# A fused attention and gated-MLP kernel: issue order and PSUM banks from a fixed table instead of a build-time search

## Chip, cores and metric

One core of one Trainium2 chip. The metric is device time in microseconds (us) for one execution; the kernel before takes 921.35 us, the median of three runs (919.81 to 922.08). "fp32r" in the rows is the float32 form that most matmuls use here; a value is split into a rounded high part and the rest as a low part, and products of the parts are added.

## What is computed

```python
def _attn_ref(q, k, v):                       # 4 x 8 heads, 1152 keys, head size 64
    q_pool = q.reshape(B, H, S // 2, 2, D).mean(axis=3)
    scores = (1 / sqrt(D)) * q_pool @ k.T     # 576 queries per head
    scores = scores - max(scores, axis=-1)
    attn = exp(scores) / (sum(exp(scores)) + 1e-09)
    return attn @ v
def _moe_ref(x, w_gate, w_val, w_out):        # 2304 tokens, 512 -> 1536 -> 512
    return (1 / (1 + exp(-(x @ w_gate))) * (x @ w_val)) @ w_out
```

`x` is the attention output with the heads of one batch side by side. Everything is float32 at the interface.

## The kernel before, in words

Work is cut by batch (4), head (32, numbered u) and half of the queries (2 halves of 288 columns, called g). For every head: Q and K are loaded (L442, L439), two queries are added (L455), Q and K are rounded to a high part on ScalarE (L460, L475), the low parts are made on GpSimd or VectorE (L465, L481). A first product of the high parts (`maxima`, L504; `first_head`, L412 for head 0) serves only to find each query's maximum: VectorE reduces every 128x384 block of it (L510, L417), and the negated maxima become a diagonal matrix (L335, L338) that is part of the second operand pair. Then comes the true score product, two matmuls of 288 columns per chunk of 128 keys (L610), and the exponential on ScalarE (L614).

In heads 0 to 7 (`WHOLE`) the exponentials stay in float32 and go straight into the value product (L628). In heads 8 to 31 the exponential is taken twice, rounded into `eh` (L614) and unrounded into the bank itself (L643), VectorE subtracts the two into `el` (L646), and the value product is one matmul for each (L653, L657); the sum of the exponentials is collected on GpSimd (L675, L682, L685), split (L723, L726) and multiplied with ones on TensorE (L730). The pair of heads is then normalised (L748 to L757) and split into `x` (L767, L771).

After a batch's heads comes its gated MLP (`gated`), whose products are 12 matmuls of 288 columns each (L846): gate and value per 128 features (tanh on L889, product on L895, split on L899 and L903), then three passes over the output weights (L929, L931) and the store (L942). The weights are converted once, during the first batch's MLP and the heads before it (`convert`, L785 to L811), stored to DRAM and loaded again for every batch (L862). The MLP of batch b is interleaved with the attention of batch b+1, so that TensorE always has something to do; only the last batch's MLP stands alone at the end.

At the start TensorE has 18 warm-up steps of four matmuls of 128x192 on constants (L951), whose results nobody reads. They have no input but `sel` (L990, L991).

The order of all this isn't written out. `Plan.op` registers 7153 steps, each with an engine, a planned duration, a due time and what it comes after: 3141 for TensorE, 1703 for ScalarE, 1348 for VectorE, 624 for GpSimd, 337 for the SyncE queue (loads and stores). A `Hold` is a use of a buffer slot by a group of steps; `SLOTS` says how many slots a tag has. The tag `b` is the eight PSUM banks, one of which a step must take before its first matmul; 1448 holds share them. `Plan.run` is a list scheduler over these steps: it keeps a clock and a busy time for each engine, lets each engine start the ready step that is due first, makes a step visible to other engines a fixed latency later (`LAT`), and gives a taken bank the slot that has been free longest. `Plan.search` repeats it 30 times with shaken due times and keeps the earliest end. The kernel then issues every step in the order found:

```python
    order = pl.search(30, 30.0, 1.0)
    with tc.manual_schedule():
        for o in order:
            o.fn()
```

Each engine works through its own instructions strictly in that order. The waits between engines are added when the program is built, from what each instruction reads and writes; so another order changes which waits there are, not what is computed.

Of the kernel before, what the change touches and what calls it, by code (L numbers as in the profile page):

```python
# [3 lines left out]

# [16 lines left out]

class Op:
    def __init__(self, eng, dur, fn, prio, after=(), take=None, late=0.0, keep=0.0, behind=None):
        self.eng, self.dur, self.fn, self.prio = eng, dur, fn, prio
        self.after = [a for a in after if a is not None]
        self.take, self.late, self.keep = take, late, keep
        self.users, self.start, self.end, self.behind, self.next = [], None, None, behind, []


class Hold:


    def __init__(self, tag, first=None):
        self.tag, self.slot, self.ops = tag, None, []


class Plan:


    WAIT = 0.4
    LAT = {"PE": 0.2, "ACT": 0.16, "DVE": 0.14, "POOL": 0.1, "SP": 0.0}

    def __init__(self, slots, free_order=()):
        self.free_order = free_order
        self.ops = []
        self.slots = slots
        self.holds = {t: [] for t in slots}
# [4 lines left out]
        return h  # L54

    def op(self, eng, dur, fn, prio, after=(), uses=(), take=(), late=0.0, keep=0.0, behind=None):
        o = Op(eng, dur, fn, prio, after, list(take), late, keep, behind)
        for h in uses:
            if behind is None:
                o.after.append(h.ops[0])  # L60
        for h in list(take) + list(uses):
            h.ops.append(o)
        self.ops.append(o)
        return o

    def search(self, rounds, width, shift):
        dice = random.Random(1)
        best = self.run()
        end = max(o.end for o in best)
        made = [(o, o.start, o.end) for o in best]  # L70
        slots = [(h, h.slot) for hs in self.holds.values() for h in hs]
        for _ in range(rounds):
            at = dice.uniform(-width, end)
            near = [(o, o.prio) for o, s, _ in made if at <= s <= at + width and o.eng != "SP"]
            for o, p in near:
                o.prio = p + dice.uniform(-shift, shift)
            order = self.run()
            new = max(o.end for o in order)
            if new <= end:
                best, end = order, new  # L80
                made = [(o, o.start, o.end) for o in best]
                slots = [(h, h.slot) for hs in self.holds.values() for h in hs]
            else:
                for o, p in near:
                    o.prio = p
        for o, a, b in made:
            o.start, o.end = a, b
        for h, s in slots:
            h.slot = s
        return best  # L90

    def run(self):
        n_dep = {}
        ready = {e: [] for e in self.LAT}
        for o in self.ops:
            o.users, o.next = [], []
        for k, o in enumerate(self.ops):
            o.key = (o.prio, k)
            o.at = 0.0
            n_dep[o] = len(o.after)  # L100
            for a in o.after:
                a.users.append(o)
            if o.behind:
                n_dep[o] += 1
                o.behind.next.append(o)
        free = {t: [(0.0, s) for s in range(n)] for t, n in self.slots.items()}
        nxt = {t: 0 for t in self.slots}
        left, of = {}, {}
        for t, hs in self.holds.items():
            for k, h in enumerate(hs):  # L110
                h.k, h.end = k, 0.0
                left[h] = len(h.ops)
                for o in h.ops:
                    of.setdefault(o, []).append(h)
        for o in self.ops:
            if n_dep[o] == 0:
                heapq.heappush(ready[o.eng], (o.key, o))
        busy = {e: 0.0 for e in self.LAT}
        done, order, t = 0, [], 0.0
        times = [0.0]  # L120
        heapq.heapify(times)
        seen = set()

        def can(o, t):
            for h in o.take:
                n = sum(g.tag == h.tag for g in o.take) if h.tag in self.free_order else 1
                if (h.tag not in self.free_order and nxt[h.tag] != h.k) or sum(f <= t + 1e-9 for f, _ in free[h.tag]) < n:
                    return False
            return True

        while done < len(self.ops):
            if not times:
                left = sorted((o.key[0], o.eng) for e in ready for _, o in ready[e])
                raise RuntimeError(f"planner stuck at {t}: {left[:10]} {nxt}")
            t = heapq.heappop(times)
            while times and times[0] <= t + 1e-9:
                heapq.heappop(times)
            again = True
            while again:
                again = False  # L140
                for e in self.LAT:
                    if busy[e] > t + 1e-9:
                        continue
                    put, pick, soon = [], None, []
                    while ready[e]:
                        it = heapq.heappop(ready[e])
                        o = it[1]
                        if o.at <= t + 1e-9 and can(o, t):
                            pick = o
                            break  # L150
                        if t < o.at <= t + self.WAIT and can(o, o.at):
                            soon.append(o)
                        put.append(it)

                    if pick and e != "PE" and any(
                        t + pick.dur > u.at + self.WAIT and u.prio < pick.prio - 0.3 for u in soon
                    ):
                        heapq.heappush(ready[e], it)
                        pick = None
                    for it in put:  # L160
                        heapq.heappush(ready[e], it)
                    if pick is None:
                        continue
                    o = pick
                    for h in o.take:
                        h.slot = min((s for s in free[h.tag] if s[0] <= t + 1e-9), key=lambda s: s[0])[1]
                        free[h.tag] = [s for s in free[h.tag] if s[1] != h.slot]
                        nxt[h.tag] += 1
                    o.start, o.end = t, t + o.dur
                    busy[e] = o.end  # L170
                    order.append(o)
                    done += 1
                    again = True
                    heapq.heappush(times, o.end)
                    av = o.end + self.LAT[e] + o.late
                    for h in of.get(o, ()):
                        left[h] -= 1
                        h.end = max(h.end, av + o.keep)
                        if left[h] == 0:
                            free[h.tag].append((h.end, h.slot))  # L180
                            heapq.heappush(times, h.end)
                    for u in o.users + o.next:
                        n_dep[u] -= 1
                        u.at = max(u.at, o.end if u.behind is o or u.eng == e and not o.late and e != "SP" else av)
                        if n_dep[u] == 0:
                            heapq.heappush(ready[u.eng], (u.key, u))
                            heapq.heappush(times, u.at)
        return order


@with_exitstack
def attention_glu_kernel(ctx: ExitStack, tc: tile.TileContext, qT, kT, vt_in, v, wg, wv, wo, out):
    nc = tc.nc
    B, H, D = 4, 8, 64
    SK, SQ = 1152, 576
# [4 lines left out]
    GN = 288  # L200
# [8 lines left out]
    pl = Plan(SLOTS, ("b",))  # L209
# [6 lines left out]
    late = ctx.enter_context(ExitStack())  # L216
    first = ctx.enter_context(ExitStack())
# [18 lines left out]
    def change_first():  # L236
# [10 lines left out]
    rc = const.tile([128, GN // 32], F32, name="rc")  # L247
# [5 lines left out]
    TL = {  # L253
        "b": [bank[:, 512 * i:512 * i + 512] for i in range(SLOTS["b"])],

        "K": list(zip(SK_T("KA"), SK_T("KB"))),
        "Q": list(zip(SQ_T("QA"), SQ_T("QB"))),
        "kr": tiles("kr", [128, SK], F32),
        "qr": tiles("qr", [64, 2, SQ], F32),

        "vr": tiles("vr", [128, NC, D], F32),
# [735 lines left out]
    for k in range(SLOTS["Q"]):  # L997
        for t in TL["Q"][k]:
            nc.vector.memset(t[:, SQ:SQ + 64].bitcast(F32), 0.0)
    order = pl.search(30, 30.0, 1.0)  # L1000
    with tc.manual_schedule():
        for o in order:
            o.fn()
# [34 lines left out]
```

## Time and profile before

| what | value |
| --- | --- |
| median of three runs | 921.35 us (919.81 to 922.08) |
| profiled execution: span, first to last instruction | 919.1 us |
| profiled execution: time outside the span | not shown by the page; the median is 2.3 us above this span |
| TensorE matmul busy | 910.0 us, 99% |
| TensorE weight loads busy | 882.8 us, 96% |
| GpSimd, ScalarE, VectorE busy | 671.1, 657.5, 649.5 us |
| DMA | 166.27 MB, mean 181 GB/s |

A row of a profile names the line, the engine, the operation, the tile written and the tiles read. PE is TensorE, PEld its weight loads, ACT ScalarE, DVE VectorE, POOL GpSimd, SPq the queue that issues DMAs. Matmuls overlap each other: one takes about 0.3 us from start to end while the next starts 0.13 us behind it, so a wait of TensorE that is shorter than that doesn't show as idle time. To find such waits one multiplies the number of matmuls of a stretch by the distance at which they start when nothing holds them up, and subtracts.

### The profile page before, as it was taken

What the parts mean: (1) busy time and instruction counts of PE and PEld (TensorE: products, weight loads), DVE (VectorE), ACT (ScalarE), POOL (GpSimd) and SP (SyncE); (2) the same over time, 40 slices, a digit from 0 to 9 for tenths busy, and PEclk for the clock granted to TensorE, in tenths of its full rate; (3) what the DMA queues carried; (4) which work ended last, traced back from release to release, by engine and by line L of the source; (5) the groups of instructions that cost most, each with busy time, mean ns of one, the idle gap of its engine ahead of it and who ended that gap; (6) DMA issues with size and microseconds to landing.
All of it is one profiled execution on the core that took longest, in us unless ns stands there. A gap on an engine that the chain in (4) does not pass through costs nothing.

```text
span 919.1 us, 18605 instructions
## 1 busy us (share of the span) xinstructions
PE 910.0 (99%) x6371; PEld 882.8 (96%) x6371; DVE 649.5 (71%) x1427; ACT 657.5 (72%) x1703; POOL 671.1 (73%) x669
## 2 busy tenths in 40 slices
PE   8999999999999999999999999999999999999998
PEld 8888888999999999999999999999999999999998
DVE  6677779888898987878787878877777874510112
ACT  4798899989998886777887677677877767422111
POOL 6765366889888989889899888888889877521211
PEclk9999999999999999999999999999999999999999
DMA  6899888788868666555644455554545423435432
GB/s 140 212 289 247 275 254 261 239 266 273 262 210 275 206 202 192 161 157 149 166 136 142 131 157 157 160 148 132 166 123 158 142 93 115 166 139 183 162 115 75
DMA packets 57616, 166.27 MB, mean 181 GB/s; under 512 B 17393, under 2 KB 21745, under 8 KB 51377
## 3 DMA queue, kind: packets, MB, share of 16 engines
q1 hardware_dynamic: 57360, 164.78, 59.3%
q8 instruction: 50, 0.82, 0.4%
q10 hardware_dynamic: 160, 0.30, 0.1%
q14 instruction: 46, 0.37, 0.1%
HBM read 132.12 MB, written 23.59 MB: 169 GB/s over the span
## 4 chain that ended last, share of the span: by engine, by line
PE 91%; ACT 4%; DVE 3%; POOL 1%; DMA 1%; issue 1%; POOLq 0%; ACTq 0%; DVEq 0%
PE bank L846 47%; PE bank L610 15%; PE bank L504 7%; PE bank L628 7%; PE bank L657 6%; PE bank L653 6%; PE bank L730 1%; DVE pm L417 1%; PE bank L951 1%; DMA wg<-wg_d 1%; ACT eh L614 1%; ACT bank L643 0%; ACT KA L475 0%; DMA wo<-wo_d 0%; DVE el L646 0%
## 5 line engine op out<-in xcount | busy, mean ns | idle before, releaser
L846 PE MATMUL bank<-x,wg 128*128 128x288 f32 x2304 | 353.8, 295 | 0.0
L846 PEld LDWEIGHTS bank<-x,wg 128*128 128x128 f32 x2304 | 325.6, 188 | 1.1 <-ACT sg L889 0.4
L646 DVE TENSOR_TENSOR el<-bank,eh 128x288 fp32r<-128x288 f32 x432 | 192.9, 452 | 70.7 <-ACT bank L643 65.9
L510 DVE TENSOR_REDUCE pm<-bank 128x1 f32<-128x384 f32 (+1 forms) x375 | 199.7, 550 | 49.6 <-PE bank L504 45.0
L614 ACT ACTIVATE eh<-bank 128x288 fp32r<-128x288 f32 x432 | 176.4, 409 | 73.1 <-PE bank L610 65.9
L643 ACT ACTIVATE bank<-bank 128x288 f32<-128x288 f32 x432 | 176.9, 410 | 0.2
L610 PE MATMUL bank<-QA,KA 128*128 128x288 f32 x576 | 175.1, 308 | 1.5 <-DVE pm L510 0.9
L610 PE MATMUL bank<-QB,KB 128*128 128x288 f32 x576 | 167.4, 295 | 0.0
L903 POOL TENSOR_TENSOR g<-sg,g 128x288 fp32r<-128x288 f32 x96 | 79.9, 833 | 105.2 <-ACT g L899 102.7
L675 POOL TENSOR_TENSOR acc<-acc,eh 128x576 f32<-128x576 f32 x92 | 132.5, 1440 | 16.7 <-ACT eh L614 14.6
L846 PE MATMUL bank<-g,wo 128*128 128x288 f32 x864 | 139.2, 295 | 0.2
L657 PE MATMUL bank<-el,vt 128*128 128x288 f32 x432 | 127.2, 296 | 0.5 <-DVE el L646 0.5
L653 PE MATMUL bank<-eh,vt 128*128 128x288 f32 x432 | 127.3, 296 | 0.0
L846 PEld LDWEIGHTS bank<-g,wo 128*128 128x128 f32 x864 | 125.0, 188 | 1.2 <-DMA wo<-wo_d 0.3
L504 PE MATMUL bank<-KA,QA 128*128 128x384 f32 (+1 forms) x375 | 125.7, 350 | 0.2
L610 PEld LDWEIGHTS bank<-QA,KA 128*128 128x128 f32 x576 | 108.2, 188 | 5.9 <-DVE pm L510 1.3
L610 PEld LDWEIGHTS bank<-QB,KB 128*128 128x128 f32 x576 | 108.3, 188 | 1.3
L895 DVE SCALAR_TENSOR_TENSOR sg<-sg,bank 128x288 f32<-128x288 f32 x96 | 43.3, 451 | 81.2 <-PE bank L846 79.2
L657 PEld LDWEIGHTS bank<-el,vt 128*128 128x128 f32 x432 | 81.1, 188 | 1.5 <-DVE el L646 1.2
L653 PEld LDWEIGHTS bank<-eh,vt 128*128 128x128 f32 x432 | 81.1, 188 | 0.7 <-ACT eh L614 0.3
L675 POOL TENSOR_TENSOR acc<-eh,eh 128x576 f32<-128x576 f32 x48 | 68.7, 1431 | 15.6 <-ACT eh L614 10.9
L628 PE MATMUL bank<-e,ve 128*128 128x288 f32 x288 | 76.6, 407 | 0.0
(86 smaller groups left out, 1359.6 us busy)
## 6 DMA issues: line engine op xcount, KB each, us to landing
wg<-wg_d SPq DMA_DIRECT2D x48, 1024.0 KB, 5.2
wo<-wo_d SPq DMA_DIRECT2D x36, 512.0 KB, 3.9
kr<-in_kT_dram SPq DMA_DIRECT2D x62, 288.0 KB, 5.0
wg_d<-cs SPq DMA_DIRECT2D x24, 512.0 KB, 5.0
qr<-in_qT_dram SPq DMA_DIRECT2D x31, 288.0 KB, 4.1
KP<-KA SPq DMA_DIRECT2D x30, 288.0 KB, 4.4
vr<-in_v_dram SPq DMA_DIRECT2D x24, 288.0 KB, 3.1
cr<-in_wg_dram SPq DMA_DIRECT2D x12, 512.0 KB, 5.3
```

Of the source, the lines that this page charges most:

```text
L504: nc.tensor.matmul(out=tl(m)[LO if t == 4 else ALL, 0:384], lhsT=lhs(t), rhs=rhs()[:, j * 384:(j + 1) * 384], start=True, stop=True)
L510: nc.vector.tensor_reduce(out=o, in_=tl(m)[p, 0:384], axis=AXX, op=ALU.max)
L610: nc.tensor.matmul(out=tl(m)[:, 0:GN], lhsT=tl(hd["k"])[k][:, ks], rhs=tl(hd["q"])[k][:, a:b], start=(k == 0), stop=(k == 1))
L614: nc.scalar.activation(out=ev(), in_=tl(m)[:, 0:GN], func=ACTF.Exp, scale=1.0 / 16.0)
L628: nc.tensor.matmul(out=tl(av[0])[:, 0:GN], lhsT=pair(c, 0), rhs=tl(h), start=(c == 0), stop=(c == NC - 1))
L643: nc.scalar.activation(out=p, in_=p, func=ACTF.Exp, scale=1.0 / 16.0)
L646: nc.vector.tensor_tensor(out=tl(el), in0=tl(m)[:, 0:GN], in1=ev().bitcast(F32), op=ALU.subtract)
L653: nc.tensor.matmul(out=tl(av[0])[:, 0:GN], lhsT=pair(c, w), rhs=ev(), start=(c == 0), stop=(c == NC - 1))
L657: nc.tensor.matmul(out=tl(av[1])[:, 0:GN], lhsT=pair(c, 1 - w), rhs=tl(el), start=(c == 0), stop=(c == NC - 1 and not mine_c))
L675: nc.gpsimd.tensor_tensor(out=tl(acc), in0=tl(old).bitcast(F32), in1=tl(eh).bitcast(F32), op=ALU.add)
L846: nc.tensor.matmul(out=ps[:, 0:GN], lhsT=l, rhs=r, start=(n == 0 and j == 0), stop=(n == 3 and j == 2))
L903: nc.gpsimd.tensor_tensor(out=g[:, 1, a:b], in0=tl(sg), in1=g[:, 0, a:b].bitcast(F32), op=ALU.subtract)
```

## The change

The scheduler (`search`, `run`, the durations and latencies in it) goes. What it found is replaced by two compressed tables in the source: `ORDER`, the 7153 numbers of the steps in the order in which they are issued, and `PLACES`, the slot of each of the 3069 holds. No step is added or dropped, and no instruction, shape, buffer or number of slots is changed.

```diff
-import heapq
-import random
+import base64
+import zlib
...
+ORDER = (
...
+)
+PLACES = (
...
+)
 class Op:
-    def __init__(self, eng, dur, fn, prio, after=(), take=None, late=0.0, keep=0.0, behind=None):
...
+    def __init__(self, eng, fn, after=()):
+        self.eng, self.fn, self.after = eng, fn, [a for a in after if a is not None]
...
     def op(self, eng, dur, fn, prio, after=(), uses=(), take=(), late=0.0, keep=0.0, behind=None):
-        o = Op(eng, dur, fn, prio, after, list(take), late, keep, behind)
-        for h in uses:
-            if behind is None:
-                o.after.append(h.ops[0])
+        o = Op(eng, fn, list(after) + [behind])
...
-    def search(self, rounds, width, shift):
...
-    def run(self):
...
+    def placed(self):
+
+        order = [self.ops[k] for k in unpack(ORDER, "H")]
+        holds = [h for t in self.slots for h in self.holds[t]]
+        for h, s in zip(holds, unpack(PLACES, "B"), strict=True):
             h.slot = s
-        return best
...
+        assert len(set(order)) == len(self.ops) == len(order)
+        assert all(h.slot < self.slots[h.tag] for h in holds)
         return order
+
+
+def unpack(text, kind):
+    return list(memoryview(zlib.decompress(base64.b85decode(text))).cast(kind))
...
-    order = pl.search(30, 30.0, 1.0)
+    order = pl.placed()
```

Unpacked and laid beside the list that the search of before gives, the tables say this. Slots: of the 1448 bank holds 160 keep their bank; every hold of every other tag keeps its slot. Order within an engine: 125 of TensorE's 3141 steps keep their place, 219 of ScalarE's 1703, 195 of VectorE's 1348, 75 of GpSimd's 624, 94 of the SyncE queue's 337. Half of the steps move by no more than 7 places on TensorE, 2 on ScalarE, VectorE and GpSimd, 1 in the SyncE queue; the farthest move 56, 57, 36, 41 and 16 places.

## Rows read from the trace of the kernel before

**Rows 1.** The page: span, and busy time, share and instructions by engine.
```profile
span 919.1 us, 18605 instructions
...
PE 910.0 (99%) x6371; PEld 882.8 (96%) x6371; DVE 649.5 (71%) x1427; ACT 657.5 (72%) x1703; POOL 671.1 (73%) x669
```
**Rows 2.** Chain that ended last, in order of time: start us, us, what.
```profile
23.68 1.21 PE bank L504 x7
...
28.65 2.91 PE bank L628 x12
...
798.75 117.15 PE bank L846 x882
...
915.93 0.46 DVE opart L931
```
**Rows 3.** Stretches, TensorE alone: window, its length, busy (matmuls), PEclk, DMA share, GB/s.
```profile
16.60:160.00 143.40, 141.85 (x754) 1.00 0.87 248
160.00:798.70 638.70, 637.11 (x4653) 1.00 0.58 175
...
480.00:620.00 140.00, 139.81 (x1028) 1.00 0.51 150
```
**Rows 4.** The same stretches, matmuls of line 504 alone.
```profile
16.60:160.00 143.40, 40.44 (x123) 1.00 0.87 248
160.00:798.70 638.70, 95.52 (x297) 1.00 0.58 175
...
480.00:620.00 140.00, 22.48 (x70) 1.00 0.51 150
```
**Rows 5.** The same, line 628 alone.
```profile
16.60:160.00 143.40, 76.63 (x288) 1.00 0.87 248
```
**Rows 6.** Who TensorE's weight loads waited for: us in total, times, longest us.
```profile
PEld bank L730 <- POOL dh L726: 1.4, 3, 0.7
PEld bank L610 <- DVE pm L510: 1.3, 2, 1.1
PEld bank L657 <- DVE el L646: 1.2, 3, 0.6
...
PEld bank L610 <- ACT sg L889: 0.6, 2, 0.3
```
**Rows 7.** Line 481 by engine: duration ns min/median/max, first and last start, form.
```profile
L481 POOL TENSOR_TENSOR KB<-kr,KA x46: 1404/1428/2048, 20.7 to 717.6; 64x576 fp32r<-64x576 f32 x46
L481 DVE TENSOR_TENSOR KB<-kr,KA x16: 755/963/1925, 323.5 to 727.3; 64x576 fp32r<-64x576 f32 x16
```
**Rows 8.** The page's groups: line, engine, operation, count, busy us, mean ns, idle before.
```profile
L614 ACT ACTIVATE eh<-bank 128x288 fp32r<-128x288 f32 x432 | 176.4, 409 | 73.1 <-PE bank L610 65.9
L643 ACT ACTIVATE bank<-bank 128x288 f32<-128x288 f32 x432 | 176.9, 410 | 0.2
```
**Rows 9.** Timeline of the head: start us, us, engine, line, operation.
```profile
2.27 1.25 SPq L356 DMA_DIRECT2D kr<-in_kT_dram  x2
...
2.73 7.01 PE L951 MATMUL bank<-sel 128*128 128x192 f32 x32 [2.73 <-DVE sel L991]
...
5.26 0.52 ACT L373 ACTIVATE QA<-qr 64x384 fp32r<-64x384 f32 x1 [2.43 <-DVE qr L370]
...
6.06 0.55 DVE L378 TENSOR_TENSOR QA<-qr,QA 64x384 fp32r<-64x384 f32 x1
...
7.05 0.68 ACT L389 ACTIVATE KA<-kr 128x576 fp32r<-128x576 f32 x1 [0.43 <-DMA kr<-in_kT_dram]
...
9.58 0.72 PE L412 MATMUL bank<-KA,QA 128*128 128x384 f32 x3
...
9.98 4.32 DVE L417 TENSOR_REDUCE pm<-bank 128x1 f32<-128x384 f32 x9 [3.37 <-PE bank L412]
...
14.61 0.72 DVE L335 TENSOR_TENSOR QB<-ident,pm 64x192 fp32r<-64x192 f32 x2
...
14.88 1.93 PE L951 MATMUL bank<-sel 128*128 128x192 f32 x16
...
16.65 0.31 PE L610 MATMUL bank<-QA,KA 128*128 128x288 f32 x1
```
**Rows 10.** A bank's release at 155 us: the last reduction, and the matmul behind it.
```profile
154.46 0.52 DVE L510 TENSOR_REDUCE pm<-bank 128x1 f32<-128x384 f32 x1
...
155.04 0.41 PE L610 MATMUL bank<-QA,KA 128*128 128x288 f32 x1 [0.88 <-DVE pm L510]
```
**Rows 11.** Loads of the gate weights (`wg`), 780 to 919 us.
```profile
DMA to landing us min/median/max: 4.6/4.7/5.0
```

More of the change, by code (lines that the diff above doesn't have):

```diff
@@ new lines @@
+PLACES = (
+    "c-rljS&ke>3`DsE$@|~fFH(a2BS0hB62`E*r+TSOF0n9sB3qGDd$ZRSwHdtir1+jv&h~ALvTG;$VtP7)yTOK4U9WEBm5fW}#%}6PvsITpicUfu"
+    "F_f85XpRrmyXwnW%H&m%A(xg^(*#eq8)9+tNWg9N(g5{urR}70#gM06Jey_S<H%S<wo5go$xaFFE{P+n=*!uzNL978G1E#uvFYTMF&6sFax$?I"
+    "WOG-^ofqUVb^sH8&UFl{HH2PB6o4(U1yr#DX|M{buodipo+w)9Gq)mW8CppJW1@^sT@blQ1nun7mbIb6um<0VGiNMlVU9o;Y>&+43-CcoF$kl>"
+    "oTsB%vo5r6*~YE**$GHF$%7_90Xr%YHIErIfNE&3)#DJ_X;*fJ@uoFTFr9fr%*HUVb=V*v5EYu>c4xdoDvh&D9Z|4w(wbh}1x+-GQ&Js9U`c`C"
+    "wTz;1r?8!{E&V$$*^xDjA<Rc3OO;|^1_UrnTS5@@f{)a5qOoALl`A4Wo<XchZowNl?4x6eap<%L4Rq_v5<OrR9PqH?Z^HUjl?}}djk5tCj5q;Z"
+    "%i80IAsItLe`We<4ROM{MZ8jDLCi_@b2?nnq-E%*Jmb~&72$7!P(P5H7zi~rtb-fgb8S#Ac2EaLfs$ckTYe=2BGWdZ5@SRq>y2~UtYb3BvEJMZ"
+    "9|s6@X{%c`JY<``@qCTu!W}#yBB{y;L-=f=@_JGjT`UN1z<l#7Cd}IR<CO-ewLX_%$LYX`P<9Ye-dz^)3vM3+*KcSSk$0U8E`Sb1pAu9K4{W|8"
+    "iYx@vAk?2%oWrMs4=Fr1F6TH~5Q*fpXO|`zd@#tQoTrLeKr|-PX|1T)c#fksIspTY-2&0fudq9(2;JwGuAK^Q0FOU#gGEK8G?7T~1|HVAQy>2O"
+    "?)vY3U}6{U|H$<f@Bi1o<@#Yif2!v<rtSR*e45vv#PLmB9G-u^|3mu!_5A4Z`u!*WGSvGm|GRm9>E9pUgd1T"
+)
@@ L32, with __init__ @@
+class Op:
+    def __init__(self, eng, fn, after=()):
+        self.eng, self.fn, self.after = eng, fn, [a for a in after if a is not None]
 class Hold:
-    def __init__(self, tag, first=None):
+    def __init__(self, tag):
         self.tag, self.slot, self.ops = tag, None, []
 class Plan:
-    WAIT = 0.4
-    LAT = {"PE": 0.2, "ACT": 0.16, "DVE": 0.14, "POOL": 0.1, "SP": 0.0}
     def __init__(self, slots, free_order=()):
-        self.free_order = free_order
         self.ops = []
@@ L64, in op @@
         return o
-    def search(self, rounds, width, shift):
[L67 to L88, printed above, removed]
-            h.slot = s
-        return best
@@ L92, in run @@
-    def run(self):
[L93 to L187, printed above, removed]
-        return order
```

151 lines of the change are left out of this document (147 added, 4 removed).

## The prediction

> **What bounds the kernel now.** First the page's first block [rows 1]: TensorE is busy 910.0 of 919.1 us, every other engine under 675. So TensorE's work is the floor, and only its waits can be won. Busy time hides them, because matmuls overlap; they have to be counted. The chain of waits gives the pace with nothing in the way [rows 2]: 882 matmuls of 288 columns in 117.15 us, 0.1328 each; seven maximum products (line 504) in 1.21 us, 0.173 each; twelve float32 records of line 628 in 2.91 us, 0.2425 each.
>
> Now the stretches [rows 3 to 5]. From 16.6 to 160 us: 123 x 0.173 + 288 x 0.2425 + the other 343 x 0.1328 = 21.3 + 69.8 + 45.6 = 136.7 us of work in 143.4, so 6.7 us of waits. From 160 to 798.7 us: 297 x 0.173 + 4356 x 0.1328 = 51.4 + 578.5 = 629.9 in 638.7: 8.8 us. After that the 882 run without a wait, and one VectorE instruction and a store end the program. All that a better order can win behind the head is thus 15.5 us, 1.7%. A quiet stretch shows what this traffic costs at best: from 480 to 620 us 70 x 0.173 + 958 x 0.1328 = 139.3 of 140, 0.7 us of waits, 0.005 for each us.
>
> The list of who waited for whom [rows 6] names no main culprit: GpSimd's split of the sums, maximum reductions, the subtraction into `el`, an activation that frees a bank; one to three times each, 0.2 to 1.1 us a time. A planned order met an engine that was late. One reason for lateness stands in the rows: the subtraction on line 481 takes VectorE 755 to 1925 ns and GpSimd 1404 to 2048 ns for one shape [rows 7].
>
> The Trainium skill, SBUF — State Buffer, Who interferes with whom, says that a VectorE instruction with two inputs in SBUF and a GpSimd instruction that reads SBUF shut each other out. The two ranges agree with that.
>
> **The change, part by part.** Instructions and buffers stay, so TensorE's work stays: 136.7, 629.9 and 117.2 us in the three stretches, and the head's. Everything is order, and I take it by stretches.
>
> *The head loses.* In the table all 18 warm-up steps (72 matmuls) stand ahead of TensorE's first maximum product; before, eight did, and the other ten lay between and behind the maximum products. Those ten are 40 matmuls. The last 16 take 16.65 - 14.88 = 1.77 us, 0.11 each; the first 32 take 9.58 - 2.73 = 6.85, 0.214 each [rows 9]. So the first maximum product moves from 9.58 to 9.58 + 40 x 0.11 = 14.0 us. The chain behind it is VectorE's: a reduction starts 0.40 after the first product, nine take 4.32, the diagonal ends at 15.33, 1.03 after them [rows 9]. That gives 14.0 + 0.4 + 4.32 + 1.03 = 19.75, and head 0's score product starts at about 19.85 instead of 16.65: plus 3.2 us. (It is not the full 4.4, because now the product is ready at 15.4 and waits for the last 16 warm-ups.) Bounds: nothing, if something else that the trace doesn't show sets the start, to 40 x 0.214 = 8.6 less 1.2 = 7.4 if the later warm-ups keep the early pace. I take 3.2, since the 0.11 comes from a row of the same matmul behind the first 32, where these will stand.
>
> The rest of the head is covered by that. The second part of Q is loaded behind two K halves, 1.25 us of the queue [rows 9], and ScalarE rounds both K halves before Q. So Q's rounding (0.52) starts at about 7.7 instead of 5.26 and its low part (0.55) is ready at 8.3: still 5.7 us ahead of 14.0. With fewer warm-ups in front it would cost up to 1.7. The first weight loads and K of head 1 move a few places in the SyncE queue; their users on ScalarE and GpSimd now stand where those engines wait for the late head.
>
> *The distances grow.* Between a chunk's score product and the value matmul that needs its exponential lies TensorE work, added up at the paces above. In heads 8 to 31 its median goes from 2.7 to 8.6 us for the high part and from 3.0 to 6.6 for the low part, whose fifth percentile goes from 2.3 to 3.6; from the last `acc` work to the ones product it goes from 6.2 to 7.3. A lateness of the kind in rows 6, up to 1.1 us, then no longer reaches TensorE. *The banks get closer.* The same measure between the matmul that fills a bank for its last reader and the one that overwrites it: before, 55 reuses behind the head lie under 1.1 us, and now 139. What is the least that works? From a product's start to its reduction 0.40, the reduction 0.55, then 0.06 to the next matmul [rows 9, 10]: 1.01 us, or 0.84 behind the product's own 0.173. Most of the close reuses stand at 0.9 to 1.1: enough when the reader is idle, not when it is busy.
>
> What is late next is therefore a reader of a bank. Bounds for both stretches: all 15.5 us won, or nothing and more waits at the banks. From 160 us on I take the quiet stretch's rate, 638.7 x 0.005 = 3.1 us left of 8.8: a gain of 5.7, because that stretch has the same engines and work and the longer distances. From 16.6 to 160 us I take half way between 6.7 and the quiet rate (0.7), so 3.7 left and 3.0 won, because there the value products of heads 0 to 7 still stand close behind their exponentials.
>
> *One reader per bank* I cost at nothing: two activations that take turns at one bank, and write it, need 409 and 410 ns, as long as each other [rows 8], and nothing is split that would shorten them. The Trainium skill, PSUM — Partial Sum Buffer, PSUM bank collisions raise a hardware error, says that the chip doesn't make a second engine wait at a bank but reports an error; by it too this part gives 0.
>
> *The last stretch* is TensorE alone. A gate weight's load stands at least 12 us of TensorE work ahead of its user before, 6.4 us in the table, and lands in 4.6 to 5.0 us [rows 11]: covered by 1.4. If that cover were gone four loads would cost about 1 us each. I take 0.
>
> Sum: + 3.2 - 3.0 - 5.7 + 0 = -5.5 us. The profiled span would be 913.6. The page gives no time outside the span; the median is 2.3 us above it, and I carry that over: 921.35 - 5.5 = 915.85, so 915.8 us. Three runs of the kernel before differ by 0.25%, and about 0.3% (2.8 us) is what can be told from no change: 918.6 and 924.1.
>
> **The rivals.**
>
> *The waits only move.* For it: TensorE's slack is small everywhere, and a longer distance to the exponential fills the four `el` slots, so that VectorE's subtraction waits for line 657 with maximum reductions queued behind it. Against: [rows 6] show that the named waits are few and single. If 11 of the 15.5 us stay, the gain of 4.5 less the head's 3.2 gives 920.
>
> *The banks decide, and it gets slower.* Place: the close reuses, 102 of them under 1.0 us in the table (33 before). Price: 0.3 us for each that meets a busy reader, as `sg` on line 889 costs now (0.6 us in 2 waits) [rows 6]. It decides from 28 such meetings on (28 x 0.3 = 8.4 = 5.5 + 2.8). With 45 it is 915.8 + 13.5 = 929. For it: VectorE and ScalarE are busy 71% of the time [rows 1]. Against: they work in the fixed order of the same table, so that most close reuses should meet an idle reader.
>
> *The head costs nothing*, for a start that is set by something else, or warm-ups that fit into time already lost: 915.8 - 3.2 = 912.6. Against it is the chain in rows 9, which has no other late input.
>
> *The weights land late* in the last stretch: + 4, so 920.
>
> *The table isn't followed*, since waits added at build time undo it: 921.35. Little speaks for that: issue order within an engine is kept as given.
>
> **How the numbers follow.** My forecast (911 to 918.6) 0.55; the head for nothing 0.10; waits that only move 0.15, late weights 0.04, a table without effect 0.02 (all near no change); banks 0.14. Faster is 0.65, same 0.21, slower 0.14. Eight in ten lie from 910.5 (about 0.06 below, the head free and nearly all waits gone) to 923.5 (0.14 above, the banks). The forecast's own range is 911 to 918.6.
>
> **What would show it.** In the profile after, head 0's first score product (line 610) starts near 19.9 us, with 72 warm-up matmuls in a row ahead of the first product of line 412. From 160 us to the last stretch the count of matmuls at the same paces leaves 2 to 4 us of waits, from the head to 160 us about 4. TensorE's waits for GpSimd (line 730) and `el` (line 657) are gone; what is left names VectorE or ScalarE freeing a bank. The last stretch still runs at 0.133 a matmul. I'm wrong if line 610 starts before 18 us, if the waits from 160 us on are over 6 us, or if the list of TensorE's waits is led by bank releases in the dozens.

## The result and the profile after

The kernel after takes 928.69 us (median of four runs, 927.81 to 929.55); before has 921.50 beside it, and the ratio is 1.0086 (95% interval 1.0072 to 1.0101). Timed once more beside before it was 930.08 and 1.0099 (1.0086 to 1.0112). The change makes the kernel slower, by 0.9%. The forecast of 915.8 was wrong in sign; the time lies above its range (911 to 918.6) and above the wider one that ended at 923.5.

The page of after, its first lines, against [rows 1]:

```profile
span 926.2 us, 18578 instructions
...
PE 912.4 (99%) x6371; PEld 883.6 (95%) x6371; DVE 651.8 (70%) x1427; ACT 651.8 (70%) x1703; POOL 668.2 (72%) x669
```

The work is the same; the span has 7.1 us more. Line numbers of after are 40 higher: 412 is 452, 504 is 544, 610 is 650, 628 is 668, 951 is 991, and so on. The stretches of [rows 3], TensorE alone, for after:

```profile
16.60:160.00 143.40, 140.92 (x750) 0.99 0.86 246
160.00:798.70 638.70, 633.94 (x4611) 1.00 0.56 172
```

Lines 544 and 668 have the same 123, 297 and 288 matmuls in them as in [rows 4, 5]. By the same paces the first stretch has 7.3 us of waits (6.7 before) and the second 638.7 - 51.4 - 4314 x 0.1328 = 14.4 (8.8 before). So the stretch that was to give 5.7 us took 5.6. The rest of the 7.1 us is the head's, less what the first stretch gained behind it. The head's timeline in after, against [rows 9]:

```profile
2.73 11.34 PE L991 MATMUL bank<-sel 128*128 128x192 f32 x72 [2.73 <-DVE sel L1031]
...
7.80 1.66 DVE L418 TENSOR_TENSOR QA<-qr,QA 64x384 fp32r<-64x384 f32 x1
...
13.91 1.40 PE L452 MATMUL bank<-KA,QA 128*128 128x384 f32 x7
...
14.48 4.27 DVE L457 TENSOR_REDUCE pm<-bank 128x1 f32<-128x384 f32 x9 [5.02 <-PE bank L452]
...
18.33 0.29 PE L650 MATMUL bank<-QA,KA 128*128 128x288 f32 x1
...
19.05 0.72 DVE L375 TENSOR_TENSOR QB<-ident,pm 64x192 fp32r<-64x192 f32 x2
...
19.83 0.61 PE L650 MATMUL bank<-QB,KB 128*128 128x288 f32 x1 [1.20 <-DVE QB L375]
...
20.23 0.44 PE L650 MATMUL bank<-QA,KA 128*128 128x288 f32 x1
...
20.47 0.44 PE L650 MATMUL bank<-QB,KB 128*128 128x288 f32 x1
```

The 72 warm-ups stand in one row, the first maximum product comes at 13.91, the first matmul of the score pair at 18.33, and the second, which needs the diagonal, at 19.83. In before that one is

```profile
16.80 0.30 PE L610 MATMUL bank<-QB,KB 128*128 128x288 f32 x1
```

Then something that wasn't forecast: matmuls of 288 columns start 0.24 us apart, not 0.133. Windows of after, TensorE alone, show the granted clock (the fourth column):

```profile
14.00:20.00 6.00, 3.67 (x17) 0.95 0.79 217
20.00:23.00 3.00, 3.00 (x13) 0.53 0.13 39
```

TensorE was busy 3.67 of 6 us while it waited for VectorE's reductions, and then the clock was granted at 0.53 over the next 3 us, about the lower of its two levels (1.2 of 2.4 GHz). The eleven matmuls from 20.23 to 22.91 cost 11 x 0.11 = 1.2 us more than at full clock.

Who TensorE's weight loads waited for in after, against [rows 6]:

```profile
...
PEld bank L886 <- DVE el L686: 2.6, 5, 0.8
PEld bank L544 <- DVE pm L550: 2.2, 4, 1.0
...
PEld bank L544 <- DVE el L686: 1.2, 4, 0.5
PEld bank L650 <- DVE el L686: 1.2, 3, 0.7
PEld bank L544 <- DVE opart L971: 0.9, 1, 0.9
...
PEld bank L770 <- POOL dh L766: 0.2, 1, 0.2
```

GpSimd is nearly gone from the list (1.4 us in [rows 6]), as are the waits of line 697 for `el`, as forecast. Added up over the trace from 24 us on, the weight loads' waits for ScalarE fall too, from 4.9 to 1.9 us; those for VectorE rise from 3.9 to 11.5. Many of these are of matmuls of other lines that wait for `el`. They don't read `el`: they overwrite the bank that VectorE reads to make it.

Why is VectorE late? One such wait in after, in the timeline:

```profile
314.29 1.43 POOL L715 TENSOR_TENSOR acc<-acc,eh 128x576 f32<-128x576 f32 x1 [0.72 <-ACT eh L654]
314.47 1.86 DVE L505 TENSOR_TENSOR QA<-qr,QA 64x576 fp32r<-64x576 f32 x1
...
316.43 0.45 DVE L686 TENSOR_TENSOR el<-bank,eh 128x288 fp32r<-128x288 f32 x1
...
316.93 0.43 PEld L886 LDWEIGHTS bank<-x,wg 128*128 128x128 f32 x3 [0.81 <-DVE el L686]
```

GpSimd begins an addition; 0.18 us later VectorE begins a subtraction with two SBUF inputs and takes 1.86 us where 0.75 is its least. The subtraction into `el` behind it comes 1.1 us late, and the bank it reads is the one that TensorE needs. The durations of these instructions in after (ns, min/median/max), against [rows 7]:

```profile
L505 DVE TENSOR_TENSOR QA<-qr,QA x16: 751/916/1869, 314.5 to 735.8; 64x576 fp32r<-64x576 f32 x16
...
L521 DVE TENSOR_TENSOR KB<-kr,KA x16: 755/1387/1793, 321.1 to 733.1; 64x576 fp32r<-64x576 f32 x16
```

Line 521's median was 963 and is 1387. The other line in before:

```profile
L465 DVE TENSOR_TENSOR QA<-qr,QA x16: 751/770/1736, 319.3 to 718.8; 64x576 fp32r<-64x576 f32 x16
```

Laid beside GpSimd's rows, 25 of the 32 instructions (lines 505 and 521) take over 0.8 us in after, and 17 in before (lines 465 and 481). Every one of these began while a GpSimd instruction was running, and ended 0.61 to 0.62 us behind that one's end. What the 32 take beyond 0.75 us each adds up to 14.0 us in after and 7.6 in before: in the new order more of them meet GpSimd.

### The profile page after: what moved, and what is told of

Its sections match the earlier page's. It is cut to its first block, busy times and chain, and to the rows that moved or that the text cites. A ratio compares the mean times of both kernels' runs of the same rounds, so it can differ in the third digit from the quotient of the medians.

```text
span 926.2 us, 18578 instructions
## 1 busy us (share of the span) xinstructions
PE 912.4 (99%) x6371; PEld 883.6 (95%) x6371; DVE 651.8 (70%) x1427; ACT 651.8 (70%) x1703; POOL 668.2 (72%) x669
## 4 chain that ended last, share of the span: by engine, by line
PE 90%; DVE 5%; DMA 2%; ACT 1%; issue 1%; POOL 0%; SPq 0%; DVEq 0%; POOLq 0%
PE bank L886 46%; PE bank L650 16%; PE bank L544 8%; PE bank L668 8%; PE bank L693 6%; PE bank L697 6%; PE bank L770 1%; DVE el L686 1%; DMA qr<-in_qT_dram 1%; DVE pm L550 1%; DVE KB L521 1%; DVE QA L505 1%; DMA wo<-wo_d 1%; DVE pp L550 0%; DMA vr<-in_v_dram 0%
## 5 line engine op out<-in xcount | busy, mean ns | idle before, releaser
L886 PE MATMUL bank<-x,wg 128*128 128x288 f32 x2304 | 372.6, 296 | 1.2 <-DVE el L686 1.1
L886 PEld LDWEIGHTS bank<-x,wg 128*128 128x128 f32 x2304 | 331.5, 188 | 3.4 <-DVE el L686 1.9
L654 ACT ACTIVATE eh<-bank 128x288 fp32r<-128x288 f32 x432 | 169.8, 409 | 85.4 <-PE bank L650 64.5
L686 DVE TENSOR_TENSOR el<-bank,eh 128x288 fp32r<-128x288 f32 x432 | 186.5, 450 | 58.1 <-ACT bank L683 38.5
L683 ACT ACTIVATE bank<-bank 128x288 f32<-128x288 f32 x432 | 167.6, 406 | 0.2
L544 PE MATMUL bank<-KA,QA 128*128 128x384 f32 x375 | 124.8, 355 | 2.4 <-DVE pm L550 1.3
L697 PE MATMUL bank<-el,vt 128*128 128x288 f32 x432 | 114.9, 296 | 0.0
L693 PE MATMUL bank<-eh,vt 128*128 128x288 f32 x432 | 110.8, 296 | 0.4 <-DVE el L686 0.4
L929 ACT ACTIVATE sg<-bank 128x288 f32<-128x288 f32 x96 | 38.9, 410 | 62.3 <-PE bank L886 59.7
L715 POOL TENSOR_TENSOR acc<-eh,eh 128x576 f32<-128x576 f32 x48 | 68.7, 1431 | 14.4 <-ACT eh L654 11.2
L521 POOL TENSOR_TENSOR KB<-kr,KA 64x576 fp32r<-64x576 f32 x46 | 65.8, 1434 | 18.0 <-ACT KA L515 14.0
```

The costliest lines, as they stand in the source:

```text
L544: nc.tensor.matmul(out=tl(m)[LO if t == 4 else ALL, 0:384], lhsT=lhs(t), rhs=rhs()[:, j * 384:(j + 1) * 384], start=True, stop=True)
L654: nc.scalar.activation(out=ev(), in_=tl(m)[:, 0:GN], func=ACTF.Exp, scale=1.0 / 16.0)
L683: nc.scalar.activation(out=p, in_=p, func=ACTF.Exp, scale=1.0 / 16.0)
L686: nc.vector.tensor_tensor(out=tl(el), in0=tl(m)[:, 0:GN], in1=ev().bitcast(F32), op=ALU.subtract)
L693: nc.tensor.matmul(out=tl(av[0])[:, 0:GN], lhsT=pair(c, w), rhs=ev(), start=(c == 0), stop=(c == NC - 1))
L697: nc.tensor.matmul(out=tl(av[1])[:, 0:GN], lhsT=pair(c, 1 - w), rhs=tl(el), start=(c == 0), stop=(c == NC - 1 and not mine_c))
```

## The experiments

Two theories for the stretch from 160 us on: VectorE instructions that GpSimd holds up (called the port below, for the access to SBUF that the two would share), and banks that are reused too soon; for the head, the warm-ups in front. In the expectations the waits from 160 us on were put at 13 us for after, each matmul's own distance being compared with its pace; the count used in this text gives 14.4 for the same profile. Their close reuses, 116 and 54, count the value product's second bank from its own first matmul on, where the prediction's 139 and 55 took it with the first bank.

**Warm-ups back between the maximum products** (`e1_warm_back`, on after)

```diff
+    for at, ks in moved:
+        for n, k in enumerate(ks):
+            order.remove(pl.ops[k])
+            order.insert(order.index(pl.ops[at]) + 1 + n, pl.ops[k])
```

`moved` puts steps 9 to 18 behind eight of the maximum products; they write banks 4 and 5, which are free there.

> The table of after with one thing undone: warm-up steps 9 to 18 stand again between the maximum products of head 0. Theory (the head pays for the warm-ups in front): the first product of the maxima starts near 9.6 us instead of 13.9, the first score pair runs near 16.5 instead of 19.8, the granted clock stays at 1.00 from 14 to 23 us, and the time falls by 3.2 to 4.6, from 928.7 to about 924.5. The waits from 160 us on stay at about 13 us. Rival (the order of the rest was made for a late head, so that an early head only waits later): 928 to 929.

Measured: 925.15, ratio 1.0058 (1.0045 to 1.0070), so 0.3 to 0.4% less than after. Its windows, TensorE alone:

```profile
14.00:20.00 6.00, 5.78 (x40) 1.00 0.86 215
20.00:23.00 3.00, 2.79 (x15) 1.00 0.17 50
```

and its stretches:

```profile
16.60:160.00 143.40, 142.46 (x770) 1.00 0.89 250
160.00:798.70 638.70, 633.45 (x4608) 1.00 0.55 172
```

The clock stays up, and the waits from 160 us on stay at 14.8: the rival falls. The score pair's second matmul runs at 16.99, though, 0.2 us later than in before. VectorE's diagonal holds it up; on GpSimd runs

```profile
13.79 2.93 POOL L521 TENSOR_TENSOR KB<-kr,KA 64x576 fp32r<-64x576 f32 x2 [2.13 <-ACT KA L515]
```

and beside it on VectorE

```profile
15.09 1.85 DVE L375 TENSOR_TENSOR QB<-ident,pm 64x192 fp32r<-64x192 f32 x2
```

The diagonal takes 1.85 us instead of 0.72, beside two subtractions of GpSimd that the new order puts there.

**Warm-ups in front, alone** (`b1_warm_front`, on before)

```diff
     order = pl.search(30, 30.0, 1.0)
+    warm_up = [o for o in order if o.eng == "PE" and o.prio < -4.0 and o.prio >= -5.0 and o.fn.__name__ == "busy"]
+    at = order.index(warm_up[0])
+    order = [o for o in order[:at] if o not in warm_up] + warm_up + [o for o in order[at:] if o not in warm_up]
```

> The kernel before with one thing of the change: all 18 warm-up steps ahead of the first maximum product; banks and the rest of the order stay. Theory: the first score product starts near 19.8 us instead of 16.65, TensorE's clock falls while it waits, 3.2 to 4.6 us slower: about 925.5. Rival (the rest of the head takes up the delay): 921 to 922.5.

Measured: 924.93, ratio 1.0049 (1.0037 to 1.0062). Its windows, TensorE alone:

```profile
14.00:20.00 6.00, 5.06 (x17) 0.84 0.13 41
20.00:23.00 3.00, 3.00 (x12) 0.50 0.02 5
```

and its timeline of TensorE:

```profile
18.00 0.57 PE L610 MATMUL bank<-QA,KA 128*128 128x288 f32 x1
19.12 0.58 PE L610 MATMUL bank<-QB,KB 128*128 128x288 f32 x1 [0.55 <-DVE QB L335]
19.49 0.44 PE L610 MATMUL bank<-QA,KA 128*128 128x288 f32 x1
```

The second matmul of the score pair starts at 19.12 (16.80 in before), 2.3 us late, and the clock is down. This part of the change costs 4.5 us by itself (0.0049 x 921; 3.4 to 5.7 by the interval). The clock didn't fall in every execution: in two of the five its mean was 1.000, and they took 923.4 and 923.9 us; in the other three it was 0.996, and they took 924.9 to 925.6. With before at 920.0 beside them the delay alone costs about 3.6 us, and the lower clock 1.7 more.

**One-input instructions in place of the 32 subtractions** (`e2_one_input` on after, `b2_one_input` on before)

```diff
+                if by == "DVE":
+                    e.tensor_reduce(out=tl(kh)[1][HI, s], in_=tl(kr)[HI, s].unsqueeze(2), axis=AXX, op=ALU.max)
+                    return
...
+            if on == "DVE":
+                e.tensor_reduce(out=qa[HI, 0:SQ], in_=tl(qr)[:, 0].unsqueeze(2), axis=AXX, op=ALU.max)
+                return
```

> The table of after; VectorE's low parts of Q and K in heads 16 to 31 (32 instructions that read two SBUF tiles) are replaced by a reduction over one element with one SBUF input, as long and in the same place; so those low parts are left out. Theory (these instructions are held up by GpSimd, and the reductions queued behind them release banks late): they take 0.75 us each with hardly any spread, the waits of TensorE from 160 to 800 us fall from 13 to about 7, and the time by 5 to 7, to about 922.5. Rival (the banks are too close by themselves): the waits stay within 1.5 us of 13, 927 to 929.

> Control for e2_one_input: the kernel before with the same 32 instructions of VectorE made one-input (those low parts left out). If held-up VectorE instructions cost before little because its banks are farther apart, the time falls by 0.5 to 1.5, to 919; if they cost the same in both orders, it falls by 5 to 7, to 914, and the port isn't what the change made worse.

Measured: e2_one_input 921.27, ratio 1.0014 (1.0000 to 1.0028), 0.7 to 0.85% under after. b2_one_input 916.67, ratio 0.9962 (0.9949 to 0.9975), 3.7 us under before. In e2_one_input the instructions read (ns, min/median/max):

```profile
L525 DVE TENSOR_REDUCE KB<-kr x16: 749/750/752, 320.5 to 726.1; 64x576 fp32r<-64x576 f32 x16
```

```profile
L506 DVE TENSOR_REDUCE QA<-qr x16: 746/747/749, 315.0 to 728.7; 64x576 fp32r<-64x576 f32 x16
```

and its second stretch, and that of b2_one_input:

```profile
160.00:798.70 638.70, 638.11 (x4665) 1.00 0.56 175
```

```profile
160.00:798.70 638.70, 637.99 (x4677) 1.00 0.57 175
```

In e2_one_input the waits there are 7.2 us against 14.4. The spread of 1.1 us is gone with the second SBUF input: 746 to 752 ns. So what holds these instructions up is what GpSimd does at the time, and it costs half of after's waits. In before the same edit takes the waits from 8.8 to 5.7. Both expectations for the control were off: not 1 and not 6 us, but 3.7. The port cost before 3.1 us of waits and after 7.2.

Two things come along with the edit. GpSimd is relieved as well: its busy time falls from 668.2 to 656.2 us on after and from 671.1 to 658.0 on before. And the reduction doesn't read ScalarE's rounded part, for which VectorE idled 1.8 us ahead of these 32 instructions in after and at most 0.6 in before. So the 3.1 and 7.2 us hold these shares as well as that of VectorE's hold-ups.

The Trainium skill, SBUF — State Buffer, Who interferes with whom, says that on trn2 a `tensor_reduce` never contends with GpSimd and a `tensor_tensor` with two SBUF inputs does, the loser being shut out for the other's whole instruction. The rows agree: no spread in the one, up to 1.2 us in the other, within the 1.43 us of a GpSimd instruction, and ends that follow GpSimd's.

**The bank that has been free longest** (`e3_banks_oldest`, on after; `e23`, on e2_one_input)

```diff
-            h.slot = s
+            h.slot = s   # for tag "b": of the banks free at this place of the order, the one released first
```

The edit is another `PLACES` table; 1276 of 1448 bank holds change, and no step moves.

> The order of after; each PSUM bank hold gets the bank that has been free longest in that order (1276 of 1448 holds change). By the measure of the prediction the reuses under 1.1 us behind the head go from 116 to 53; before has 54. Theory of the banks: the waits from 160 to 800 us fall from 13 to about 8, time about 924. Theory of the shared port: the late VectorE instruction stays, and a longer distance takes 0.3 to 0.5 us off each of a dozen waits at most: 925 to 928. If order alone decides: 928.7.

> e2_one_input and e3_banks_oldest together, on the table of after (the 32 low parts left out). If close banks cost only where a held-up VectorE instruction meets them, the banks add little once it is gone: waits from 160 us on at 5 to 6 us (e2_one_input has 6.4), ratio 0.999 to 1.001. If close banks cost by themselves: another 2 to 3 us less, waits at 3 to 4, ratio about 0.998.

Measured: e3_banks_oldest 922.51, ratio 1.0030 (1.0017 to 1.0043); e23 916.02, ratio 0.9948 (0.9936 to 0.9961). Their second stretch, e3_banks_oldest and then e23:

```profile
160.00:798.70 638.70, 634.67 (x4640) 1.00 0.56 174
```

```profile
160.00:798.70 638.70, 637.96 (x4697) 1.00 0.56 175
```

That is 10.6 and 3.0 us of waits, the maximum products being 297 in each. Banks take off 3.8 with the port's trouble (14.4 to 10.6) and 4.2 without it (7.2 to 3.0). The time of e3_banks_oldest, too, is nearer to what the theory of the banks gave (924) than to that of the port (925 to 928). So close banks cost by themselves, and the first reading in the expectation of e23, that they only hurt where a held-up instruction meets them, falls.

Not all of the 0.6% in e3_banks_oldest's median is the banks'. In its profile the clock stayed up in the head:

```profile
14.00:20.00 6.00, 4.22 (x18) 1.00 0.89 235
20.00:23.00 3.00, 3.00 (x19) 1.00 0.24 66
```

Its mean was 1.000 in three of its six executions and in none of after's eight. At the same mean of 0.996, two of its executions took 923.3 and 925.5 us, and four of after's 929.6 to 930.4.

**Both undone** (`c1_both`: e1_warm_back, and the oldest bank from the first score products on; `c2_both_trim`: the last five warm-up steps left out too)

```diff
-            for _ in range(4):
+            for _ in range(4 if k < 13 else 0):   # c2_both_trim alone
```

> The order of after with both undone: ten warm-ups back between the maximum products, and from the first score products on the bank that has been free longest. If the head's loss and the banks' loss are two separate things, their gains of 2.7 and 5 us add up: about 920.5, ratio to before 1.000 to 1.001, with the waits of the head as in e1_warm_back (4.1 us) and those from 340 us on as in e3_banks_oldest (7.4). If one hides the other: 922 to 923.

> c1_both with the last five warm-up steps left out (nobody reads them). The first score pair no longer waits for them: up to 1 us earlier, about 919.5, ratio 0.998 to 1.000. Rival: VectorE's diagonal sets the start, or TensorE's clock falls in the gaps: the same as c1_both or 1 us more.

Measured: c1_both 920.48, ratio 1.0003 (0.9994 to 1.0012); c2_both_trim 920.27, 1.0004 (0.9995 to 1.0013). The two gains add up: with these two parts undone the time is that of before again. That doesn't mean that nothing else in the table costs: the port's part stays (24 of the 32 subtractions still take over 0.8 us), and up to 160 us the new order has fewer waits (3.7 us against 6.7).

Without the last warm-ups nothing is won, as the rival had it. The profile of c2_both_trim (an execution of 922.29 us, 2.0 above its median) shows both of the rival's reasons. First the diagonal:

```profile
15.17 2.87 POOL L521 TENSOR_TENSOR KB<-kr,KA 64x576 fp32r<-64x576 f32 x2 [2.96 <-ACT KA L515]
...
15.66 2.59 DVE L375 TENSOR_TENSOR QB<-ident,pm 64x192 fp32r<-64x192 f32 x2
...
18.31 0.52 PE L650 MATMUL bank<-QB,KB 128*128 128x288 f32 x1 [3.08 <-DVE QB L375]
```

The pair's first matmul starts at 14.94 (17.12 in c1_both), but the second at 18.31 (17.67 in c1_both). Then the clock; its windows, TensorE alone:

```profile
14.00:20.00 6.00, 2.92 (x14) 0.87 0.71 182
20.00:23.00 3.00, 3.00 (x14) 0.69 0.59 171
```

TensorE was busy for 2.92 of 6 us, and the lower clock followed; in c1_both, with the last warm-ups in place, it was busy for 5.78, and the clock stayed at 1.00. How much each of the two costs isn't shown.

**The kernel after once more** (`a0_after`)

> The kernel after once more, beside the next three on one chip: 1.0086 times before, so about 928.

Measured: 930.08, 1.0099; given above.

**Fewer subtractions on VectorE, whole computation** (`b3_k_pool` and `b4_q_pool` on before, `c3_all` on c1_both)

```diff
-    KLD = lambda u: u >= 16
+    KLD = lambda u: False              # b3_k_pool, c3_all
-    QLP = lambda u: 1 <= u < 2 * H
+    QLP = lambda u: 1 <= u             # b4_q_pool
```

> The kernel before, whole computation, with the low part of K in heads 16 to 31 on GpSimd instead of VectorE (16 instructions of 1.42 us), the search of before free to place them. If half of the 3.7 us that b2_one_input gained comes back and GpSimd has room (88% busy from 340 us on): about 918.5, ratio 0.998. If GpSimd becomes what the sums and the split of the gate wait for: 921 to 924.

> The kernel before, whole computation, with the low part of Q in heads 16 to 31 on GpSimd instead of VectorE, the search free to place them. As for b3_k_pool: about 918.5 if the port is all that counts, 921 to 924 if GpSimd's longer queue counts more.

> c1_both, whole computation, with the low part of K in heads 16 to 31 on GpSimd, in the same place of the order. If the port's share of the waits (7 us from 160 us on, by e2_one_input) is half K's, it falls by 3 and the time to 917 to 918, as with b3_k_pool. If GpSimd's strict order can't take 16 more instructions without a new plan: 920 to 923.

Measured: b3_k_pool 918.11, ratio 0.9968 (0.9956 to 0.9980), faster than both kernels; b4_q_pool 920.49, 0.9995 (0.9987 to 1.0004), no change and neither of its two expectations; c3_all 922.36, 1.0016 (1.0006 to 1.0026), no faster than c1_both (the intervals overlap). In b3_k_pool, where the search made a new order, the stretch from 340 to 798.7 us:

```profile
340.00:798.70 458.70, 458.11 (x3376) 1.00 0.48 148
```

With its 211 maximum products that is 458.7 - 36.5 - 3165 x 0.1328 = 1.9 us of waits; before has 209 of 3354 matmuls there and 4.9. From 160 to 340 us, ahead of nearly all the moved instructions, it has 6.0 against 3.7, so part of its gain goes to another order there. In c3_all the order wasn't made for the move. Its weight loads waited for GpSimd:

```profile
...
PEld bank L770 <- POOL dh L766: 2.7, 5, 0.9
PEld bank L544 <- POOL QA L505: 1.8, 2, 1.6
...
PEld bank L886 <- POOL g L943: 0.8, 1, 0.8
```

## Why the prediction was wrong, point by point

*The bound* was right: TensorE's work didn't change, and the 7.1 us of span are waits and a slower clock.

*The head* was right in its chain: 13.91 for 14.0 and 19.83 for 19.85. The 19.83 is the second matmul of the pair, 3.0 us later than in before; the first doesn't need the diagonal and ran at 18.33. Q's low part was ready at 9.46 and not at 8.3, as it took 1.66 us and not 0.55, without effect on 13.91. The price was short by the clock, which the prediction left out: 3.2 us forecast, 4.5 measured alone in b1_warm_front, about 3.6 of them without a fall of the clock. Inside after, undoing it gave 2.6 to 3.8 us; there the diagonal is late beside GpSimd even with the warm-ups back, by 0.2 us against before.

*From 16.6 to 160 us* a gain of 3.0 was forecast. With the head put right (e1_warm_back: 754 matmuls before, 770 now) the waits are 4.6 against 6.7, a gain of 2.1. Right in direction.

*From 160 us on* is the step that failed: a gain of 5.7, on the ground that the stretch "has the same engines and work and the longer distances", so that a lateness of up to 1.1 us "no longer reaches TensorE", and a loss of 5.6 in fact. The lateness reached TensorE by another way: less by the value product that waits for an exponential than by the bank that VectorE frees late. The prediction's own sign of being wrong, over 6 us of waits there, came. Six profiles, with and without the port and the old bank rule, split the loss, in us of waits from 160 to 798.7:

| | port as it is | one-input instructions |
| --- | --- | --- |
| before | 8.8 | 5.7 |
| after | 14.4 | 7.2 |
| after's order, oldest bank | 10.6 | 3.0 |

Each cell is one profile. Others with the same order and bank rule there give 10.0 for before (b1_warm_front), 14.4 and 14.8 for after (a0_after, e1_warm_back), 9.5 and 10.7 for the last row (c1_both, c2_both_trim), so that a difference of about 1 us says nothing.

With port and banks out of the way the new order has 3.0 us where the old has 5.7, a gain of 2.7; that it comes from the longer distances wasn't tried by itself. They don't take up VectorE's lateness: with the old bank rule and the port as it is the new order has 10.6, no less than before's 8.8. Its bank table costs 4.2 (7.2 - 3.0), and the port costs 4.1 more than before (7.2 against 3.1). The sum, - 2.7 + 4.2 + 4.1, is the 5.6. That 3.0 is nearly the 3.1 that I had left is luck, as the 3.1 was meant for the port as it is.

I had the ground for both. The closer banks were counted and then set aside because "most close reuses should meet an idle reader". The held-up instructions were read as the reason for waits that the change would cover, not as something whose number depends on the order. The rival "the banks decide" (0.14) was right in sign, and its 929 fits by luck: it put 13.5 us on the banks (45 busy readers at 0.3 us), and they cost about 4. The rest of the way from 915.8 is the port and the gains that didn't come.

*One reader per bank* at nothing wasn't tried by itself; of the two activations in [rows 8] only line 643 writes the bank, line 614 writes `eh`. *The late weights* didn't come: TensorE shows no wait for `wg`, and two for `wo`, 0.5 us in all.

What stays open: why this order meets GpSimd more often; how its table was made isn't known here. With the head put right the durations hardly move (the mean of line 521 is 1295 ns in e1_warm_back, 1316 in after), so a late head isn't the cause.

## What to carry to other kernels

When only the order changes, set the gain from longer distances against what the order does to the resources that it shares, and price both: how soon each bank is overwritten, and which instructions of two engines overlap on a port. Choosing the bank that has been free longest adds no instruction and won 0.6 to 0.7% here, in the same order (in e3_banks_oldest a part of it through the clock). Before moving matmuls that nobody reads, look at what waits behind them, and at the clock in the gap that they leave.

## What the runs showed of the hardware

When TensorE had waited in pieces (3.67 us busy of 6 in after, 2.92 in c2_both_trim), the next 3 us had a granted clock of 0.53 and 0.69, with matmuls 0.24 us apart instead of 0.133. This didn't come every time: with 4.22 of 6 in e3_banks_oldest the clock stayed at 1.00, and the five executions of b1_warm_front went both ways.

A VectorE subtraction of 64x576 with two SBUF inputs took 751 to 1925 ns; each that took over 800 had begun while a GpSimd instruction was running, and ended 0.61 to 0.62 us behind that one's end. A one-input reduction of that shape took 746 to 752.
